# Tau-masked attention and a gated feed-forward on one core: 84 transposed tiles through the DMA crossbar instead of 70, shared staging buffers, one set of leads

## The chip, the cores and the metric

The kernel runs on one core of a Trainium2 chip. The metric is the time of one execution on the device in microseconds, the median of three runs. The kernel before takes 859.21 us (858.94 to 859.27).

## The reference

Eight batches, eight heads, 576 tokens, head size 64, all in float32. Cut to what matters:

```
scores = q @ k^T / 8                                   # per batch and head: 576 x 576
e      = where(scores >= max(scores) - tau, exp(scores - max), 0)
x      = (e / (sum(e) + 1e-9)) @ v                     # heads joined: 576 x 512 per batch
h      = relu(x @ w_in)                                # 512 -> 1024
c      = conv over tokens of h, 3 taps per channel
out    = (h * sigmoid(c)) @ w_out                      # 1024 -> 512
```

## The kernel before, in words

**Tiling.** The 576 queries of a batch are cut into four tiles of 128 and one of 64. Each batch has two chunks: the even chunk holds tiles 0 and 1, the odd chunk tiles 2, 3 and the small one, so there are 16 chunks. Heads go in four pairs per chunk. A unit (`unit`, L574) is one tile of one pair of heads; the small tiles of two neighbouring pairs are put together into one unit. That makes 8 units in an even chunk, 10 in an odd one, 18 in a batch and 144 in all; 128 of them are full tiles and 16 are small-tile units. "Half a chunk" below is the units of two pairs of heads, which end in one `attend`.

**One unit.** TensorE computes the scores of both heads into PSUM (L595). VectorE takes the row maximum (L607), ScalarE the exponential into the tile `em` (L614), VectorE the mask and the row sum (L617), and GpSimd, in one case of four ScalarE, the division (L655, L653). The keys lie along the columns of `em` and must come to the partitions before the product with v. This is done in one of two ways:

- `transposes` (L699): TensorE turns nine blocks of 128 x 128 in three groups of three (L710) into PSUM tiles `ps_t`, and ScalarE copies each group to the tile `eT` (L720). For a small-tile unit the two pairs have different `eT` tiles, so each group is copied in two halves (L726).
- `cross` (L671): the float32 words of `em` are split into their two 16-bit halves, one half by ScalarE and one by GpSimd (L363, L365), in a tile `parts`. SyncE's queue (SP) writes `parts` to a scratch tensor `rows` in DRAM (L688), and two transposing DMAs (called turns here, L695), one for each 64 rows of queries, bring them back into `eT` through the DMA crossbar.

Which way a unit goes is told by `crossed` (L666) from the table `CROSS`: for each pair of heads, the number of full tiles of a chunk that go through the crossbar (even chunks, odd chunks), and then whether the small-tile units go there. The first batch uses none. Before, that is one full tile of each pair in each chunk and all small-tile units: 10 units in a batch, 70 in all.

**Attend.** `attend` (L733) multiplies `eT` by v for two pairs of heads at a time, in two PSUM tiles of the same tag `ps_t`, and writes x (L754, L757). There are two `eT` buffers, one per pair, so the turns of the next two pairs wait until this product has read them.

**Feed-forward.** `ffn` (L839) gives the work of a finished chunk: `mm2` for blocks of 128 tokens (L827 into `po`, copied to the tile `ot` at L834, stored at L835), and `mm1` for each of eight slices of channels (L776 into `ph`, then relu, two taps, tanh and gate on ScalarE and VectorE). It is spread evenly over the units of the next chunk. What is left after the last unit ends the kernel.

**Weights.** `split` (L391) loads 16 pieces of 64-bit numbers in a `stage` buffer, converts them by way of a `value` buffer and writes a high and a low float32 part. This lies beside the first batch.

**The order.** All this is given to a planner on the host (`Plan`, L113). Each operation has a duration, a rank (its unit's number minus a lead) and its dependencies. `Plan.run` plays them on a model of the engines with a priority list and writes out one fixed order per engine; each engine then runs its order in sequence, and SP's queue does too. The leads are `AHEAD` by kind of work; `TRIM` adds to each of 12 kinds an amount for each of 16 chunks and the tail, read by `Lead` (L103). `LATENCY`, `HOLD`, `LATE`, `KEEP` and `SWITCH` are further costs of the model, `WRATE` is the rate at which weight pieces are ranked, and `BACKLOG` and `ALT` say when an operation may go to an engine other than its own. Buffers are handed out in turn: `STB`, `PTB`, `EMS`, `ETB` and `FAR` count those of `stage`, `parts`, `em`, `eT` and `rows`.

Of the kernel before, what the change touches and what calls it, by code (L numbers as in the profile page):

```python
# [22 lines left out]
AHEAD = {'mask': 5.447, 'norm': 7.929, 'parts': -2.68, 'gate': 1.222, 'evac': -0.535, 'low': 0.609, 's': 8.622, 's4': 8.87, 't': 3.177, 'a': 3.675, 'prep': 4.965, 'w': 1.618, 'load': 0.216, 'first': 3.806, 'ffn': 0.0}  # L23

TRIM = {
# [4 lines left out]
    'evac': (1.75, 1.55, -1.24, -3.99, -1.54, -1.06, 0.79, -0.48, -3.91, -4.07, -2.13, -3.07, -1.44, -1.08, -0.76, 0.84, 20.46),  # L30
    'mask': (-4.04, -1.01, 0.38, 3.13, -3.14, -4.4, -3.97, -4.18, -5.91, 0.85, 2.4, -3.79, 2.55, 0.33, -0.3, 4.2, 15.62),
    'parts': (9.64, -0.54, -1.96, -1.18, 0.42, 0.38, -0.86, 0.2, 4.19, 1.41, 3.28, -0.14, 1.44, 2.79, -0.77, 2.92, -20.75),
    'norm': (4.33, -3.3, -3.77, -0.77, 0.45, -1.05, 3.76, 0.73, -2.68, -1.39, 0.59, -0.77, -0.61, 3.7, -1.16, -2.44, 1.27),
    'gate': (-0.59, 0.08, -3.29, -0.05, -0.28, -0.05, 0.16, -0.15, -0.66, 0.11, -0.12, -0.14, -0.18, 0.76, -0.08, 1.88, -21.9),
    'low': (0.16, 0.28, -2.25, -1.71, -3.14, 3.41, 0.75, -0.39, -2.87, 2.41, -1.85, 2.2, -1.3, -0.19, -0.35, 4.7, 4.08),
    'prep': (-0.0, 0.01, 0.67, -1.53, 0.37, 1.4, 0.62, -0.62, -4.34, 0.86, -1.53, -0.82, -0.61, 1.13, -0.55, 1.19, -14.25),
    'ffn': (-4.93, 0.29, -0.2, -0.59, 0.59, -0.09, -0.24, -0.48, 0.08, -0.32, 0.15, 0.06, 0.45, -0.27, -0.0, 0.65, -9.58),
}
# [11 lines left out]
MOE = (3, 2)  # L50
BACKLOG = {'pool': 3000.0, 'dve': 3000.0, 'act': 9000000000.0}
WRATE = (1.713, 2.547)
ALT = 10.85
# [16 lines left out]
FAR = 4  # L70
# [32 lines left out]
class Lead:  # L103


    def __init__(self, plan):
        self.plan = plan

    def __getitem__(self, key):
        return AHEAD[key] + TRIM[key][self.plan.phase] if key in TRIM else AHEAD[key]  # L110


class Plan:  # L113
# [4 lines left out]
    def __init__(self):  # L118
        self.ops, self.wrote, self.read, self.bufs, self.tags, self.rank, self.phase = [], {}, {}, [], {}, 0.0, 0
# [160 lines left out]
def tile_tau_attention_gated_ffn(  # L280
# [48 lines left out]
    ahead_of = Lead(plan)  # L329
# [49 lines left out]
    def act(n, psum=False):  # L379
        return n * 0.833 + (58 if psum else 95)  # L380
# [10 lines left out]
    def split(src, n, name, high, low, hr, lr, first="load"):  # L391
# [3 lines left out]
        stage = plan.buf(wk, "stage", STB, [P, 1024], U32, name)  # L395
        value = plan.buf(wk, "value", 2, [P, 512], U32, f"{name}_f")
# [12 lines left out]
        w = ahead_of["w"]  # L409
# [20 lines left out]
        put(2 * n, load, issue=330, w=[hi, lo], r=[(gate, 0)] if first == "first" else [], ahead=w + ahead_of[first])  # L430
# [86 lines left out]
    def prep(i):  # L517
# [13 lines left out]
        a = ahead_of["prep"]  # L531
# [35 lines left out]
    def load_v(i, b, p):  # L567
        if b and chunks[pairs[i][0]].new[0]:
            return vts[i - NP]
        vt = plan.buf(wk, "v", VB, [P, NBLK, D], F32, f"v_{i}")  # L570
        put(NBLK * D, lambda: nc.sync.dma_start(vt[:], vc[b, p]), w=[(vt, 0)], r=[(gate, 0)] if i < NP else [], ahead=ahead_of["prep"])
        return vt

    def unit(u, sides, small):  # L574
# [7 lines left out]
        a = ahead_of["s4" if small else "s"]  # L582
# [48 lines left out]
        for h in range(m):  # L631
            op("dve", 738, late[h], w=[(em, h), (few, ("sum", h))], r=[(pss[h], 0), (few, "th")], ahead=a + ahead_of["mask"])
# [38 lines left out]
    def cross(u, em, dsts):  # L671

        parts = plan.buf(wk, "parts", PTB, [P, 2, 2 * S], U16, f"parts_{u}")
        rows = plan.buf(far, "rows", FAR, [2 * P, 2 * S], U16, f"rows_{u}")
        a = ahead_of["s"]
        for j in range(2):
            def part(e, j=j):
                src = em[:].bitcast(U16).rearrange("p (k two) -> p two k", two=2)[:, j]
                copy(e, parts[:, j], src)
# [3 lines left out]
            op(  # L683
                home, choice[home], part, w=[(parts, j)], r=[(em, 0), (em, 1)], ahead=a + ahead_of["parts"], port=True,
                other=[(e, ns) for e, ns in choice.items() if e != home]
            )
        put(
            864, lambda: nc.sync.dma_start(rows[:].rearrange("(q two) k -> q two k", two=2), parts[:]),  # L688
            w=[(rows, 0)], r=[(parts, 0), (parts, 1)], ahead=a, late=LATE["rows"]
        )  # L690
        for j in range(2):
            eT, g = dsts[j]

            def turn(j=j, eT=eT, g=g):
                nc.sync.dma_start_transpose(eT[:].bitcast(U16)[:, g], rows[j * P:(j + 1) * P, :])  # L695

            op("sp", 1560, turn, w=[(eT, (g, "x"))], r=[(rows, 0)], ahead=a, late=LATE["turn"], ring=1840)

    def transposes(u, em, dsts):  # L699
# [3 lines left out]
        def group(b0, n):  # L703
# [8 lines left out]
            op("pe", n * P * 0.852, turns, w=[(pt, 0)], r=[(em, 0), (em, 1), (ident, 0)], ahead=ahead_of["t"], kind="turn")  # L712
# [4 lines left out]
            if dsts[0][0] is dsts[1][0]:  # L717
# [15 lines left out]
    def attend(of, w, parts):  # L733

        pas = [plan.buf(ps_t, "ps_t", 2, [P, 512], F32, f"pa_{i}") for i, *_ in of]
        a = ahead_of["a"]
# [15 lines left out]
        for (i, p, eT, vt, x, off), pa in zip(of, pas):  # L752
# [6 lines left out]
            op("act", act(w, True), high, w=[(x, 0)], r=[(pa, 0)], ahead=a + ahead_of["low"])  # L759
            op("dve", dve(w), low, w=[(x, 1)], r=[(pa, 0), (x, 0)], ahead=a + ahead_of["low"])  # L760


    def mm1(c, f, xs):
# [23 lines left out]
        op("act", act(an, True), relu, w=[(hp, 0)], r=[(ph, 0), (hp.home, 0)], ahead=ahead_of["gate"])  # L787
        for j, k in enumerate((0, 2)):
# [4 lines left out]
            op("dve", dve(kn, 150), tap, w=[(t, 0)], r=[(hp, 0), (cr, 0)], ahead=ahead_of["gate"], port=True)  # L793
# [4 lines left out]
        op("act", act(kn) + 92, lambda: nc.scalar.activation(t[:, :kn], t[:, :kn], AF.Tanh, scale=cm[:, 0, f:f + 1]), w=[(t, 0)], r=[(cr, 0)], ahead=ahead_of["gate"])  # L798
        op("dve", dve(kn), gate, w=[(t, 0)], r=[(hp, 0)], ahead=ahead_of["gate"], port=True)
# [18 lines left out]
    def mm2(m):  # L818
# [4 lines left out]
        ot = plan.buf(wk, "ot", 2, [P, DO], F32, f"ot_{m}")  # L823
# [10 lines left out]
        op("act", act(DO, True), lambda: nc.scalar.activation(ot[:, :DO], po[:], AF.Copy), w=[(ot, 0)], r=[(po, 0)])  # L834
        put(DO, lambda: nc.sync.dma_start(tokens[m * P:(m + 1) * P, :], ot[:, :DO]), r=[(ot, 0)])  # L835
# [105 lines left out]
    plan.phase = len(chunks)  # L941
# [53 lines left out]
```

## Time and profile before

| | us |
|---|---|
| median of three runs | 859.21 (858.94 to 859.27) |
| the profiled execution | 857.69 |
| its span, first to last instruction | 855.9 |
| TensorE matmuls busy | 829.5 (97%) |
| TensorE weight loads busy (beside the matmuls) | 610.4 (71%) |
| VectorE busy | 725.4 (85%) |
| ScalarE busy | 659.3 (77%) |
| GpSimd busy | 407.3 (48%) |
| main DMA queue, share of 16 engines | 61.4% |
| granted TensorE clock, share of full speed | 1.0 in all slices |

Engines run side by side, so their times don't add up. Matmuls are pipelined: a row's duration overlaps the next one's, and what one costs the engine is the distance from its start to the start of the next. In the profile's names PE is TensorE, PEld its weight loads, DVE VectorE, ACT ScalarE, POOL GpSimd and SP SyncE. Traffic of the crossbar way: 576 KB written for each unit (70 of them) and 140 turns of 288 KB.

### The profile page before, as it was taken

Reading aid. Unit: us, or ns where it says so; the run is one execution under the profiler, and the core shown is the slowest. Engines: PE = TensorE matmul, PEld = TensorE weight load, DVE = VectorE, ACT = ScalarE, POOL = GpSimd, SP = SyncE. Lnnn points to the kernel's source line nnn. Section 1 sums busy time; section 2 is a strip of 40 time slices with the busy share of each in tenths; the row PEclk is TensorE's granted clock in tenths of the full one; section 3 lists DMA queues with packets and bytes.
Section 4 is the critical chain, followed back from the end, with each engine's and each line's share of the span. In section 5 each row is a group of like instructions: output and inputs, shape, how many; then the busy total and the mean of one; then the engine's idle time right before and its main releaser. Section 6 shows DMA issues by size and latency. Waiting matters only on the chain.

```text
span 855.9 us, 20930 instructions
## 1 busy us (share of the span) xinstructions
PE 829.5 (97%) x7710; PEld 610.4 (71%) x7710; DVE 725.4 (85%) x1869; ACT 659.3 (77%) x1300; POOL 407.3 (48%) x549
## 2 busy tenths in 40 slices
PE   6888999999999999999999999999999999999998
PEld 2545677767777677767777677776778677776896
DVE  6999889989899699987979879996979879997542
ACT  6999888877778678877878777896778768876642
POOL 3556545644537345553445445563553535554321
PEclk9999999999999999999999999999999999999999
DMA  8454247679667877668665686678665586645300
GB/s 274 152 169 153 75 120 180 170 206 206 167 145 178 216 185 189 167 184 226 164 161 130 199 200 163 150 210 229 154 167 154 167 221 176 151 124 152 80 26 37
DMA packets 213381, 140.72 MB, mean 164 GB/s; under 512 B 170400, under 2 KB 189088, under 8 KB 213280
## 3 DMA queue, kind: packets, MB, share of 16 engines
q1 hardware_dynamic: 212848, 139.09, 61.4%
q8 instruction: 61, 1.00, 0.5%
q10 hardware_dynamic: 432, 0.30, 0.1%
q14 instruction: 40, 0.33, 0.1%
HBM read 47.34 MB, written 50.72 MB: 115 GB/s over the span
## 4 chain that ended last, share of the span: by engine, by line
PE 86%; ACT 6%; DVE 5%; issue 1%; POOL 0%; DMA 0%; DVEq 0%; ACTq 0%
PE ph L776 23%; PE po L827 23%; PE ps_s L595 17%; PE pa L746 15%; PE ps_t L710 8%; ACT em L614 2%; DVE few L607 2%; DVE em L617 2%; ACT eT L720 1%; DVE t L791 1%; ACT stage_f L415 1%; PE pw_stage L441 0%; ACT stage L419 0%; DVE t L796 0%; DMA k<-in_kp_dram 0%
## 5 line engine op out<-in xcount | busy, mean ns | idle before, releaser
L655 POOL TENSOR_SCALAR em<-em,few 128x576 f32<-128x576 f32 x217 | 171.1, 796 | 215.1 <-DVE few L641 174.5
L607 DVE TENSOR_REDUCE few<-ps_s 128x1 f32<-128x576 f32 x288 | 209.2, 748 | 56.3 <-PE ps_s L595 54.4
L614 ACT ACTIVATE em<-ps_s,few 128x576 f32<-128x576 f32 x288 | 208.5, 747 | 61.7 <-DVE few L607 61.1
L617 DVE SCALAR_TENSOR_TENSOR em<-ps_s,few,em 128x576 f32<-128x576 f32 x288 | 224.9, 811 | 14.6 <-ACT em L614 7.5
L776 PE MATMUL ph<-x,w1h 128*128 128x322 f32 (+1 forms) x1024 | 237.0, 307 | 0.0
L370 POOL TENSOR_TENSOR gl<-t,gh 128x255 fp32r<-128x255 f32 (+9 forms) x192 | 121.0, 641 | 170.6 <-ACT gh L806 158.7
L776 PEld LDWEIGHTS ph<-x,w1h 128*128 128x128 f32 x1024 | 172.4, 189 | 21.4 <-issue 14.4
L595 PE MATMUL ps_s<-k,q 64*64 64x288 f32 x2048 | 163.8, 423 | 13.5 <-DVE em L617 8.3
L746 PE MATMUL pa<-eT,v 64*64 64x256 f32 (+1 forms) x2304 | 152.1, 403 | 0.0
L776 PE MATMUL ph<-x,w1l 128*128 128x322 f32 (+1 forms) x512 | 151.0, 295 | 0.0
L746 PEld LDWEIGHTS pa<-eT,v 64*64 64x64 f32 x2304 | 91.5, 133 | 48.6 <-issue 1.3
L827 PE MATMUL po<-w2h,gh 128*128 128x512 f32 x288 | 118.9, 413 | 0.0
L595 PEld LDWEIGHTS ps_s<-k,q 64*64 64x64 f32 x2048 | 67.3, 133 | 71.3 <-issue 29.5
L720 ACT ACTIVATE eT<-ps_t 128x384 f32<-128x384 f32 x216 | 101.6, 507 | 15.3 <-PE ps_t L710 15.0
L827 PE MATMUL po<-w2h,gl 128*128 128x512 f32 x288 | 112.7, 391 | 0.3 <-POOL gl L370 0.3
L827 PE MATMUL po<-w2l,gh 128*128 128x512 f32 x288 | 112.7, 391 | 0.0
L710 PE MATMUL ps_t<-ident,em 128*128 128x128 f32 x666 | 102.2, 280 | 7.0 <-POOL em L655 3.2
L710 PEld LDWEIGHTS ps_t<-ident,em 128*128 128x128 f32 x666 | 76.1, 141 | 39.5 <-ACT eT L720 11.7
L776 PEld LDWEIGHTS ph<-x,w1l 128*128 128x128 f32 x512 | 96.6, 189 | 0.4
L791 DVE SCALAR_TENSOR_TENSOR t<-hp,cr 128x321 f32<-128x321 f32 (+1 forms) x128 | 78.5, 614 | 19.4 <-ACT hp L785 18.5
L365 POOL COPY parts<-em 128x1152 uint16<-128x1152 uint16 x70 | 83.1, 1188 | 16.4 <-POOL em L655 5.5
L798 ACT ACTIVATE t<-t,cm 128x321 f32<-128x321 f32 (+1 forms) x128 | 68.4, 538 | 23.2 <-DVE t L791 16.4
(73 smaller groups left out, 941.9 us busy)
## 6 DMA issues: line engine op xcount, KB each, us to landing
rows<-parts SPq DMA_DIRECT2D x70, 576.0 KB, 3.6
q<-in_qd_dram SPq DMA_DIRECT2D x63, 256.0 KB, 3.4
v<-in_vc_dram SPq DMA_DIRECT2D x36, 288.0 KB, 4.3
out_dram<-ot SPq DMA_DIRECT2D x36, 256.0 KB, 3.1
k<-in_kp_dram SPq DMA_DIRECT2D x31, 288.0 KB, 4.0
stage<-in_w_in_dram SPq DMA_DIRECT2D x8, 512.0 KB, 4.9
stage<-in_w_out_dram SPq DMA_DIRECT2D x8, 512.0 KB, 3.9
eT<-rows SPq DMA_TRANSPOSE x140, 4.2
```

What stands on the lines that cost most here:

```text
L370: engines[e].tensor_tensor(dst, x, y, op=ALU.subtract)
L595: nc.tensor.matmul(ps[g * D:(g + 1) * D, AT + c * CH:AT + (c + 1) * CH], lhsT=q(on, h), rhs=k[on, h * CH:(h + 1) * CH], start=True, stop=True)
L607: nc.vector.tensor_reduce(few[:, nm], scores(), op=ALU.max, axis=mybir.AxisListType.XY, negate=True)
L614: nc.scalar.activation(view(), scores(), AF.Exp, bias=few[:, nm])
L617: nc.vector.scalar_tensor_tensor(view(), scores(), few[:, th], view(), op0=ALU.is_ge, op1=ALU.mult, accum_out=few[:, total])
L655: engines[e].tensor_scalar(sl, sl, LEAST, few[:, 10 + h:11 + h], op0=ALU.add, op1=ALU.mult)
L710: nc.tensor.transpose(out=pt[:, i * P:(i + 1) * P], in_=block, identity=ident[:])
L720: "act", act(n * P, True), lambda: nc.scalar.activation(eT[:, g:g + 2, b0:b0 + n, :], source(), AF.Copy),
L746: nc.tensor.matmul(pa[j * D:(j + 1) * D, :w], lhsT=vt[on, step, :], rhs=eT[on, :w // D, step, :], start=(step == 0), stop=(step == NBLK - 1))
L776: nc.tensor.matmul(ph[:, :an], lhsT=w1[w][:, cb, fs], rhs=xs[cb][:, h, :an], start=(cb == 0 and i == 0), stop=(cb == NCB - 1 and i == 2))
L791: nc.vector.scalar_tensor_tensor(t[:, :kn], hp[:, o + k:o + kn + k], cr[:, j, f:f + 1], y, op0=ALU.mult, op1=ALU.add)
L827: nc.tensor.matmul(po[:], lhsT=x[:, f, at:at + P], rhs=w[:, f, :], start=(f == 0 and i == 0), stop=(f == NFB - 1 and i == 2))
```

## The change: what it does

- `CROSS`: two full tiles of every first and third pair of heads and one of every second and fourth go through the crossbar, and no small-tile unit does. That is 12 units in a batch, 84 in all, all of them full tiles.
- The tile `parts` has no buffer of its own (before: one); it takes one of the three `stage` buffers, which grow from 1024 to 1152 words. The output tile `ot` takes a `value` buffer; these become three (before: two of `value`, two of `ot`).
- `rows` has three scratch tensors instead of four.
- `TRIM`, `Lead` and the lead `ffn` go; every lead has one value for the whole kernel. All other numbers of the planner have new values, so the order of work on every engine is a new one.

```diff
-AHEAD = {'mask': 5.447, 'norm': 7.929, 'parts': -2.68, 'gate': 1.222, 'evac': -0.535, 'low': 0.609, 's': 8.622, 's4': 8.87, 't': 3.177, 'a': 3.675, 'prep': 4.965, 'w': 1.618, 'load': 0.216, 'first': 3.806, 'ffn': 0.0}
-TRIM = {
-    's': (-0.17, 0.37, 0.28, -0.24, -0.45, -0.1, -0.02, -0.17, -0.17, -0.23, -0.12, -0.0, -0.27, 0.06, 0.05, 1.05, -19.16),
...
-LATENCY = {'pe': 205.37, 'act': 213.173, 'dve': 118.588, 'pool': 62.545, 'ring': 1882.404}
-HOLD = {'pool': 134.468, 'dve': 107.493}
+AHEAD = {'mask': 10.551, 'norm': 10.168, 'parts': -3.787, 'gate': 1.873, 'evac': 0.451, 'low': 0.345, 's': 8.614, 's4': 9.392, 't': 3.022, 'a': 3.819, 'prep': 6.275, 'w': 1.364, 'load': 0.901, 'first': 5.447}
+LATENCY = {'pe': 228.875, 'act': 210.482, 'dve': 115.463, 'pool': 47.975, 'ring': 1863.104}
+HOLD = {'pool': 114.519, 'dve': 83.078}
...
-MOE = (3, 2)
-BACKLOG = {'pool': 3000.0, 'dve': 3000.0, 'act': 9000000000.0}
-WRATE = (1.713, 2.547)
-ALT = 10.85
+MOE = (2, 1)
+BACKLOG = {'pool': 1000000000.0, 'dve': 0.0, 'act': 9000000000.0}
+WRATE = (2.137, 2.121)
+ALT = 4.72
...
-FAR = 4
+FAR = 3
...
-PTB = 1
+VAB = 3
 QB = 2
-CROSS = ((1, 1, 1, 1), (1, 1, 1, 1), (1, 1))
-LATE = {'load': 1319.0, 'copy': 4674.0, 'rows': 335.0, 'turn': -88.0}
-KEEP = {'rows': 3.322, 'cols': 0.012, 'turn': 0.252, 'full': 0.371}
+CROSS = ((2, 1, 2, 1), (2, 1, 2, 1), (0, 0))
+LATE = {'load': 1337.0, 'copy': 13931.0, 'rows': -123.0, 'turn': 157.0}
+KEEP = {'rows': 3.335, 'cols': 0.001, 'turn': 0.103, 'full': 0.266}
...
-        stage = plan.buf(wk, "stage", STB, [P, 1024], U32, name)
-        value = plan.buf(wk, "value", 2, [P, 512], U32, f"{name}_f")
+        stage = plan.buf(wk, "stage", STB, [P, 2 * S], U32, name)
+        value = plan.buf(wk, "value", VAB, [P, 512], U32, f"{name}_f")
...
-        parts = plan.buf(wk, "parts", PTB, [P, 2, 2 * S], U16, f"parts_{u}")
+        parts = plan.buf(wk, "stage", STB, [P, 2 * S], U32, f"parts_{u}")
...
-        ot = plan.buf(wk, "ot", 2, [P, DO], F32, f"ot_{m}")
+        ot = plan.buf(wk, "value", VAB, [P, DO], U32, f"ot_{m}")
...
-            plan.rank -= ahead_of["ffn"]
```

## Rows read from the trace of the kernel before

**Rows 1.** Stages, busy us of each engine (instructions), then clock, DMA share, GB/s.

```profile
0.00:105.00 105.00, 85.80 (x786) 52.61 (x787) 92.32 (x248) 91.68 (x184) 54.19 (x73) 1.00 0.52 168
105.00:800.00 695.00, 691.52 (x6596) 513.19 (x6595) 610.53 (x1580) 545.63 (x1064) 338.87 (x456) 1.00 0.68 175
800.00:856.00 56.00, 52.21 (x334) 44.62 (x332) 22.55 (x42) 21.96 (x54) 14.22 (x21) 1.00 0.07 25
...
204.00:302.00 98.00, 97.23 (x916) 71.88 (x915) 85.00 (x214) 73.15 (x144) 46.48 (x62) 1.00 0.73 177
...
700.00:800.00 100.00, 99.10 (x945) 75.10 (x946) 87.64 (x225) 77.10 (x154) 49.69 (x69) 1.00 0.61 157
```

**Rows 2.** The chain that ended last, share of the span by engine and line.

```profile
PE 86%; ACT 6%; DVE 5%; issue 1%; POOL 0%; DMA 0%; DVEq 0%; ACTq 0%
PE ph L776 23%; PE po L827 23%; PE ps_s L595 17%; PE pa L746 15%; PE ps_t L710 8%; ACT em L614 2%; DVE few L607 2%; DVE em L617 2%; ACT eT L720 1%; DVE t L791 1%; ACT stage_f L415 1%; PE pw_stage L441 0%; ACT stage L419 0%; DVE t L796 0%; DMA k<-in_kp_dram 0%
```

**Rows 3.** Waits in us (times, longest), TensorE over the span, VectorE in 105:800.

```profile
PE ps_s L595 <- DVE em L617: 9.6, 11, 2.2
...
DVE few L607 <- PE ps_s L595: 51.9, 43, 5.4
```

**Rows 4.** Timeline of TensorE around groups of transposes: start us, us.

```profile
418.67 0.87 PE L710 MATMUL ps_t<-ident,em 128*128 128x128 f32 x6
419.30 0.48 PE L827 MATMUL po<-w2h,gh 128*128 128x512 f32 x1
...
437.19 0.82 PE L710 MATMUL ps_t<-ident,em 128*128 128x128 f32 x6
437.94 1.20 PE L595 MATMUL ps_s<-k,q 64*64 64x288 f32 x16
439.08 0.55 PE L710 MATMUL ps_t<-ident,em 128*128 128x128 f32 x3
439.38 0.39 PE L776 MATMUL ph<-x,w1h 128*128 128x322 f32 x1
```

**Rows 5.** Groups of instructions: busy us, mean ns, idle before and releasers.

```profile
L655 POOL TENSOR_SCALAR em<-em,few 128x576 f32<-128x576 f32 x217 | 171.1, 796 | 215.1 <-DVE few L641 174.5 <-PE ps_s L595 19.1 <-PE ps_t L710 9.1
...
L710 PE MATMUL ps_t<-ident,em 128*128 128x128 f32 x666 | 102.2, 280 | 7.0 <-POOL em L655 3.2 <-ACT eT L720 2.4 <-DMA q<-in_qd_dram 1.2
L720 ACT ACTIVATE eT<-ps_t 128x384 f32<-128x384 f32 x216 | 101.6, 507 | 15.3 <-PE ps_t L710 15.0
...
L365 POOL COPY parts<-em 128x1152 uint16<-128x1152 uint16 x70 | 83.1, 1188 | 16.4 <-POOL em L655 5.5 <-DMA rows<-parts 2.5 <-issue 2.5
L363 ACT ACTIVATE parts<-em 128x1152 uint16<-128x1152 uint16 x70 | 81.6, 1165 | 1.6 <-POOL em L655 1.4
...
L726 ACT ACTIVATE eT<-ps_t 128x192 f32<-128x192 f32 x12 | 3.6, 393 | 0.0
```

**Rows 6.** Timeline of GpSimd and VectorE around one half of a tile's parts.

```profile
419.89 1.21 POOL L365 COPY parts<-em 128x1152 uint16<-128x1152 uint16 x1
...
417.63 0.47 DVE L791 SCALAR_TENSOR_TENSOR t<-hp,cr 128x255 f32<-128x255 f32 x1
...
420.09 1.29 DVE L791 SCALAR_TENSOR_TENSOR t<-hp,cr,t 128x255 f32<-128x255 f32 x1
```

**Rows 7.** Instructions of the weights' staging: ns min/median/max, first and last start us.

```profile
L428 POOL TENSOR_TENSOR stage_f<-stage_f,stage x16: 1284/1298/1466, 17.2 to 91.3; 128x512 int32<-128x512 int32 x16
```

**Rows 8.** Two attends in the chain, in order of time: start us, us.

```profile
407.22 4.84 PE pa L746 x72
...
424.11 3.89 PE pa L746 x72
```

**Rows 9.** SP's queue between these attends, and the turns' landing over the span.

```profile
412.10 3.02 SPq L695 DMA_TRANSPOSE eT<-rows  x2
...
415.85 3.52 SPq L695 DMA_TRANSPOSE eT<-rows  x2
...
DMA to landing us min/median/max: 3.4/4.2/6.4
```

More of the change, by code (lines that the diff above doesn't have):

```diff
@@ L100 @@
 Chunk = collections.namedtuple("Chunk", "b tiles new cols tokens done")
[L103 to L110, printed above, removed]
 class Plan:
     def __init__(self):
-        self.ops, self.wrote, self.read, self.bufs, self.tags, self.rank, self.phase = [], {}, {}, [], {}, 0.0, 0
+        self.ops, self.wrote, self.read, self.bufs, self.tags, self.rank = [], {}, {}, [], {}, 0.0
     def buf(self, pool, tag, bufs, shape, dtype, name):
@@ L389, in pool1, with split @@
         return n * 0.9 + 225
-    def split(src, n, name, high, low, hr, lr, first="load"):
-        stage = plan.buf(wk, "stage", STB, [P, 1024], U32, name)
-        value = plan.buf(wk, "value", 2, [P, 512], U32, f"{name}_f")
+    def split(src, n, name, high, low, hr, lr, lead="load"):
+        stage = plan.buf(wk, "stage", STB, [P, 2 * S], U32, name)
+        value = plan.buf(wk, "value", VAB, [P, 512], U32, f"{name}_f")
         def flat():
@@ L408, in split @@
         lo, hi, a = (stage, 0), (stage, 1), (value, 0)
-        w = ahead_of["w"]
+        w = AHEAD["w"]
         def load():
@@ L428, in f4 @@
             nc.gpsimd.tensor_tensor(v(I32), v(I32), words(I32)[0], op=ALU.add)
-        put(2 * n, load, issue=330, w=[hi, lo], r=[(gate, 0)] if first == "first" else [], ahead=w + ahead_of[first])
+        put(2 * n, load, issue=330, w=[hi, lo], r=[(gate, 0)] if lead == "first" else [], ahead=w + AHEAD[lead])
         op("act", act(n), f0, w=[a], r=[hi], ahead=w)
@@ L530, in prep @@
         q = plan.buf(wk, "q", QB, [P, 2, w], F32, f"q_{i}")
-        a = ahead_of["prep"]
+        a = AHEAD["prep"]
         after = [(gate, 0)] if i < NP else []
@@ L570, in load_v @@
         vt = plan.buf(wk, "v", VB, [P, NBLK, D], F32, f"v_{i}")
-        put(NBLK * D, lambda: nc.sync.dma_start(vt[:], vc[b, p]), w=[(vt, 0)], r=[(gate, 0)] if i < NP else [], ahead=ahead_of["prep"])
+        put(NBLK * D, lambda: nc.sync.dma_start(vt[:], vc[b, p]), w=[(vt, 0)], r=[(gate, 0)] if i < NP else [], ahead=AHEAD["prep"])
         return vt
@@ L581, in unit @@
         few.home = fews[few.turn % FEW]
-        a = ahead_of["s4" if small else "s"]
+        a = AHEAD["s4" if small else "s"]
         late, pss = [], []
@@ L631, in unit @@
         for h in range(m):
-            op("dve", 738, late[h], w=[(em, h), (few, ("sum", h))], r=[(pss[h], 0), (few, "th")], ahead=a + ahead_of["mask"])
+            op("dve", 738, late[h], w=[(em, h), (few, ("sum", h))], r=[(pss[h], 0), (few, "th")], ahead=a + AHEAD["mask"])
         ss = [(few, ("sum", h)) for h in range(m)]
@@ L671, in cross, with halves @@
     def cross(u, em, dsts):
-        parts = plan.buf(wk, "parts", PTB, [P, 2, 2 * S], U16, f"parts_{u}")
+        parts = plan.buf(wk, "stage", STB, [P, 2 * S], U32, f"parts_{u}")
+        def halves():
+            return parts[:].bitcast(U16).rearrange("p (j k) -> p j k", j=2)
         rows = plan.buf(far, "rows", FAR, [2 * P, 2 * S], U16, f"rows_{u}")
-        a = ahead_of["s"]
+        a = AHEAD["s"]
         for j in range(2):
@@ L678, in part @@
                 src = em[:].bitcast(U16).rearrange("p (k two) -> p two k", two=2)[:, j]
-                copy(e, parts[:, j], src)
+                copy(e, halves()[:, j], src)
             choice = {"act": act(2 * S), "pool": pool1(2 * S), "dve": dve(2 * S)}
@@ L683, in cross @@
             op(
-                home, choice[home], part, w=[(parts, j)], r=[(em, 0), (em, 1)], ahead=a + ahead_of["parts"], port=True,
+                home, choice[home], part, w=[(parts, j)], r=[(em, 0), (em, 1)], ahead=a + AHEAD["parts"], port=True,
                 other=[(e, ns) for e, ns in choice.items() if e != home]
@@ L687, in cross @@
         put(
-            864, lambda: nc.sync.dma_start(rows[:].rearrange("(q two) k -> q two k", two=2), parts[:]),
+            864, lambda: nc.sync.dma_start(rows[:].rearrange("(q two) k -> q two k", two=2), halves()),
             w=[(rows, 0)], r=[(parts, 0), (parts, 1)], ahead=a, late=LATE["rows"]
@@ L710, in turns @@
                     nc.tensor.transpose(out=pt[:, i * P:(i + 1) * P], in_=block, identity=ident[:])
-            op("pe", n * P * 0.852, turns, w=[(pt, 0)], r=[(em, 0), (em, 1), (ident, 0)], ahead=ahead_of["t"], kind="turn")
+            op("pe", n * P * 0.852, turns, w=[(pt, 0)], r=[(em, 0), (em, 1), (ident, 0)], ahead=AHEAD["t"], kind="turn")
             def source():
@@ L720, in group @@
                     "act", act(n * P, True), lambda: nc.scalar.activation(eT[:, g:g + 2, b0:b0 + n, :], source(), AF.Copy),
-                    w=[(eT, (g, b0))], r=[(pt, 0)], ahead=ahead_of["t"] + ahead_of["evac"]
+                    w=[(eT, (g, b0))], r=[(pt, 0)], ahead=AHEAD["t"] + AHEAD["evac"]
                 )
@@ L726, in group @@
                         "act", act(n * D, True), lambda j=j, eT=eT, g=g: nc.scalar.activation(eT[:, g, b0:b0 + n, :], source()[:, j], AF.Copy),
-                        w=[(eT, (g, b0))], r=[(pt, 0)], ahead=ahead_of["t"] + ahead_of["evac"]
+                        w=[(eT, (g, b0))], r=[(pt, 0)], ahead=AHEAD["t"] + AHEAD["evac"]
                     )
@@ L735, in attend @@
         pas = [plan.buf(ps_t, "ps_t", 2, [P, 512], F32, f"pa_{i}") for i, *_ in of]
-        a = ahead_of["a"]
+        a = AHEAD["a"]
         read = parts + [(y[3], 0) for y in of]
@@ L757, in low @@
                 nc.vector.tensor_tensor(x[:, 1, off:off + w], pa[:, :w], x[:, 0, off:off + w].bitcast(F32), op=ALU.subtract)
-            op("act", act(w, True), high, w=[(x, 0)], r=[(pa, 0)], ahead=a + ahead_of["low"])
-            op("dve", dve(w), low, w=[(x, 1)], r=[(pa, 0), (x, 0)], ahead=a + ahead_of["low"])
+            op("act", act(w, True), high, w=[(x, 0)], r=[(pa, 0)], ahead=a + AHEAD["low"])
+            op("dve", dve(w), low, w=[(x, 1)], r=[(pa, 0), (x, 0)], ahead=a + AHEAD["low"])
     def mm1(c, f, xs):
@@ L785, in relu @@
             nc.scalar.activation(hp[:, 1:1 + an], ph[:, :an], AF.Relu, scale=0.5)
-        op("act", act(an, True), relu, w=[(hp, 0)], r=[(ph, 0), (hp.home, 0)], ahead=ahead_of["gate"])
+        op("act", act(an, True), relu, w=[(hp, 0)], r=[(ph, 0), (hp.home, 0)], ahead=AHEAD["gate"])
         for j, k in enumerate((0, 2)):
@@ L833, in mm2 @@
             op("pe", 691, mm, w=[(po, 0)], r=gs + [(w, (f, i)) for w in w2 for i in range(0, DO, WN)], kind="full")
-        op("act", act(DO, True), lambda: nc.scalar.activation(ot[:, :DO], po[:], AF.Copy), w=[(ot, 0)], r=[(po, 0)])
-        put(DO, lambda: nc.sync.dma_start(tokens[m * P:(m + 1) * P, :], ot[:, :DO]), r=[(ot, 0)])
+        op("act", act(DO, True), lambda: nc.scalar.activation(ot[:, :DO].bitcast(F32), po[:], AF.Copy), w=[(ot, 0)], r=[(po, 0)])
+        put(DO, lambda: nc.sync.dma_start(tokens[m * P:(m + 1) * P, :], ot[:, :DO].bitcast(F32)), r=[(ot, 0)])
     tokens = out.rearrange("b s d -> (b s) d")
@@ L938, in tile_tau_attention_gated_ffn @@
             plan.rank, fn = work.pop(0)
-            plan.rank -= ahead_of["ffn"]
             fn()
-    plan.phase = len(chunks)
     for _, fn in work + ffn(len(chunks)):
```

19 lines of the change are left out of this document (4 added, 15 removed), and 3 rows, old and new, of the table TRIM.

## The prediction

> **What bounds the kernel now.** I read the busy times by stage first. Three stages have different limits [rows 1]. In the first 105 us, batch 0 and the weights, TensorE is busy 85.8 us, so it stands idle 19.2, while VectorE (92.3) and ScalarE (91.7) are nearly full. From 105 to 800 us, where batches 1 to 7 run, TensorE is busy 691.5 of 695 us: 3.5 us idle in all. From 800 us only feed-forward is left, and TensorE idles 3.8 us at the end. Then the chain that ended last: 86% of it is TensorE's own work, 8% of the span being the transposes [rows 2]. Last the waits: VectorE waits 51.9 us for scores in the middle stage, while TensorE's longest wait for VectorE is 9.6 us over the whole span [rows 3]. So the middle stage is set by how much work TensorE is given, and the others follow it. The clock is 1.00 in every stage [rows 1] and does not enter.
>
> The Trainium skill ("Perfetto Trace Analysis", Identifying the Most-Contended Engine) says that matmul busy time is a poor measure of how near TensorE is to its limit, and wants weight loads judged instead. By that the middle stage is at 513 of 695 us, 74%, and the matmuls taken away would buy nothing. The starts of successive matmuls leave no gap here, so I side with the chain; the rule's case comes back as a rival.
>
> **Transposes on TensorE.** Units that TensorE transposes fall from 74 to 60: 44 full tiles and all 16 small ones, against 72 and 2. At nine each that is 540 instead of the 666 of [rows 5], 126 fewer. The mean of 280 ns there is a pipelined duration; the price is the distance between starts [rows 4]: three transposes take 439.38 - 439.08 = 0.30 us, six take 419.30 - 418.67 = 0.63 us, so 100 to 105 ns each. With scores next, six take 437.94 - 437.19 = 0.75 us, 125 ns each. A removed group mostly stands between other work whose change of shape remains, so I take 102.5 ns: 126 x 0.1025 = 12.9 us, between 12.6 and 15.8. All of it is in the middle stage, and nearly all on the path.
>
> **ScalarE and GpSimd.** 84 copies of 507 ns go (216 to 132: -42.6 us), 84 half copies of 393 ns come (12 to 96: +33.0), and 14 halves of `parts` at 1165 ns come (+16.3) [rows 5]: ScalarE +6.7 us on 545.6 in the middle [rows 1]. GpSimd gets 14 x 1.188 = +16.6 us on 338.9. Both have over 140 us of room there and cost nothing while TensorE stays the last to finish. VectorE gets no new work, but an L791 step beside a `parts` copy on GpSimd took 1.29 us against 0.47 [rows 6], so I count up to 14 x 0.82 = 11.5 us: 622 of the 682 us left, 91% against 88% now. TensorE's backlog covers that; without the cover the whole 11.5 us would come back.
>
> **SP and the crossbar.** 14 more units bring 14 writes and 28 turns to SP's queue. Two turns occupy it 3.0 to 3.5 us [rows 9], so about 14 x 3.3 = 46 us more over 682, beside loads that stand in the same queue. The DMA engines are at 0.68 over the middle stage, 473 us [rows 1]. If everything there were crossbar traffic, a unit would be 473/70 = 6.8 us; at the head's rate (168 GB/s at share 0.52, so 323 GB/s when full) its 1.18 MB would be 3.7 us. So 14 units add 51 to 95 us and the share becomes 0.77 to 0.83. That is room still, and the stretch with share 0.73 leaves TensorE 0.8 us idle in 98, the one with 0.61 leaves 0.9 in 100 [rows 1]: up to here TensorE does not feel it. I take nothing, with the rival below as the other end.
>
> The small-tile units, last of their half chunk, now reach `eT` by TensorE and a half copy instead of a write and a turn, whose turn alone lands after 4.2 us [rows 9]. That eases the attends of odd chunks. In even chunks each half now needs six turns instead of four, and since `eT` has one buffer per pair they can start only after the attend before.
>
> **Buffers.** `parts` gets up to three buffers instead of one; the waits for the single one (2.5 us on GpSimd [rows 5]) lie off the path. The weights have left `stage` by 91.3 + 1.3 us [rows 7], and no unit before batch 1 uses the crossbar, so they hardly meet; outputs meet the weights in `value` even less. Three `rows` tensors are just the three units of a half chunk. All this I put at zero, between -1 and +1 us.
>
> **Edits that change nothing.** `MOE`: the list of `ffn` has put all blocks but one of `mm2` first, then the last, then `mm1`, whatever the pair. `LATE['copy']` is read nowhere. `BACKLOG` and `ALT`: of 218 divisions whose own engine is GpSimd, 217 ran there [rows 5], so hardly anything was moved.
>
> **The new order.** The trims can have improved only what was idle. In the middle that is 3.5 us at present; a perfect order would give back these 3.5, and an order as loose as the head (18% idle) would cost over 100. The middle is nearer, since the same backlog of feed-forward stands ready there, but one set of leads has less to fit with: I let the idle time double, +3.5 us. In the head weight pieces are asked for at other rates; there VectorE and ScalarE bind, and their work is the same: 0, between -4 and +6. The end is TensorE's own row of matmuls: 0.
>
> **The sum.** 857.69 (profiled execution: span 855.9 and 1.8 around it) - 12.9 + 3.5 = 848.3. The median of the runs is 859.21, 1.5 above the profiled one, so 849.8 us. Its own range: 846 to 855.
>
> **Rivals.**
>
> *Late attends (slower).* The place is the gap between the attend that ends at 407.22 + 4.84 = 412.1 and the one at 424.1 [rows 8]. Four turns go out, the last begins near 417.6 and lands near 421.8 by the median 4.2 us [rows 9], 2.3 us before its reader. Two more turns take 3.3 us, so the attend would be 1 us late, and later as the DMA share grows. TensorE runs in order, so an attend at the front of its queue holds everything. It decides from 12.9 / 28 = 0.46 us of waiting per attend of batches 1 to 7. At 0.8 us each it costs 22.4: 857.7 - 12.9 + 22.4 + 1.5 = 868.7 us. For it: the 2.3 us. Against it: no attend waits for a turn now, and the planner may place attends later, since the four gaps of a batch have about 99 - 18 = 81 us together and need some 15 each. The Trainium skill ("VectorE: DVE Perf Modes", Rules for kernel authors) speaks for it: it sends a 128 x 128 transpose to TensorE where PSUM will do, to the crossbar otherwise. The 60 x 9 transposes that stay follow it; the 14 moved units go against it.
>
> *VectorE takes the place (no change).* In the head VectorE is 88% busy and TensorE waits. If 622 us of VectorE cannot be packed closer than about 89.5%, the middle stays at 695 us and the time at 859 (855 to 861 with the packing a little off). For it: the head. Against it: VectorE's 51.9 us of waits for scores, and 87.6 of 100 us with such waits among them [rows 1, 3]. This is also the case in which the skill's weight-load rule would be right.
>
> *A loose order (slower).* Without trims TensorE idles 3% of the middle stage, 20 us: 857.7 - 12.9 + 17 + 1.5 = 863 us. For it: 204 numbers go. Against it: the backlog.
>
> *More than forecast.* Each removed group takes its change of shape with it (15.8 us), idle time stays as it is, and the head gains 4: 857.7 - 15.8 - 4 + 1.5 = 839.4; with only part of this 840 to 846.
>
> **How the numbers follow.** Forecast 0.50, more than forecast 0.16, VectorE 0.12, late attends 0.13, loose order 0.09. A measurement of this kernel tells 0.2% (1.7 us) from none, so faster means below 857.5: 0.50 + 0.16 + 0.02 of the VectorE case = 0.68; within 857.5 to 860.9: 0.08 of it and 0.01 of the loose order = 0.09; slower: 0.13 + 0.08 + 0.02 = 0.23. The range from 842 to 866 leaves out about 0.07 below and 0.10 above. The predicted time is 849.8 us.
>
> **What would show it.** 540 transposes with starts 100 to 105 ns apart; 96 half copies and 84 of each `parts` row; a middle stage shortened by 8 to 13 us with TensorE idle under 8 us in it; DMA share 0.77 to 0.83. Late attends would show as waits of L746 or its weight loads for a transposing DMA, the VectorE case as TensorE's scores waiting for L617 by over 10 us in the middle, the loose order as idle time of TensorE spread over many releasers. The prediction is wrong if the middle stage does not shrink, or if the head's 105 us change by more than 6.

## The result, and the profile after

The changed kernel takes 844.26 us (842.77 to 844.64, four runs) against 859.08 for the one before on the same chip: a ratio of 0.9824 [0.9807, 0.9841], 14.8 us less. The forecast was 849.8, the range 842 to 866. The direction and the range held; the time came out 1.7 us below the forecast's own range of 846 to 855, where the rival "more than forecast" stands. The profiled execution took 844.64 us, 13.05 less than the one before.

The stages of the changed kernel, columns as in [rows 1]; the last line is a piece of the head:

```profile
0.00:105.00 105.00, 86.56 (x750) 50.32 (x751) 93.33 (x237) 88.16 (x175) 53.55 (x72) 0.97 0.50 166
105.00:800.00 695.00, 692.75 (x6634) 509.72 (x6633) 628.70 (x1609) 555.80 (x1108) 366.52 (x482) 1.00 0.78 199
800.00:843.00 43.00, 39.00 (x205) 34.42 (x203) 14.90 (x25) 14.53 (x31) 8.77 (x10) 1.00 0.08 31
...
40.00:60.00 20.00, 17.18 (x118) 9.14 (x117) 18.30 (x53) 17.22 (x34) 9.04 (x10) 0.83 0.53 183
```

In the head TensorE is busy about as long as before (86.6 us for 85.8). Between 105 and 800 us TensorE is idle 2.25 us, less than the 3.5 of [rows 1], and does more of its work there, so that 43 us are left after 800 instead of 56. The DMA share is 0.78. In the head of this execution TensorE's clock stood at 1.2 instead of 2.4 GHz for 6.8 us, after a stretch in which TensorE idled for 1.8 of 4 us between transposes (44 to 48 us; the row of 40 to 60 shows the mean clock, 0.83). Of the four runs the only one at full clock throughout was the fastest, 842.77, against 844.2 to 844.6, so the spell costs about 1.6 us here.

The chain that ended last and the groups that answer to [rows 2] and [rows 5] (line numbers are smaller, since the trims are gone):

```profile
PE 89%; ACT 5%; DVE 4%; issue 1%; DMA 0%; POOL 0%; DVEq 0%; ACTq 0%
PE ph L754 24%; PE po L805 24%; PE ps_s L569 18%; PE pa L724 16%; PE ps_t L688 7%; DVE few L581 1%; ACT em L588 1%; ACT eT L698 1%; DVE em L591 1%; ACT stage_f L389 1%; ACT stage L393 1%; DMA k<-in_kp_dram 0%; ACT k L337 0%; ACT w1h L410 0%; ACT w2h L410 0%
...
L724 PE MATMUL pa<-eT,v 64*64 64x256 f32 (+1 forms) x2304 | 152.2, 403 | 0.7 <-ACT eT L704 0.7
...
L339 POOL COPY parts<-em 128x1152 uint16<-128x1152 uint16 x84 | 100.8, 1200 | 29.1 <-issue 18.6 <-POOL em L629 8.1
L337 ACT ACTIVATE parts<-em 128x1152 uint16<-128x1152 uint16 x84 | 98.1, 1168 | 1.2 <-POOL em L629 0.9
...
L688 PE MATMUL ps_t<-ident,em 128*128 128x128 f32 x540 | 85.4, 285 | 7.7 <-ACT eT L698 3.7 <-POOL em L629 2.5 <-DMA q<-in_qd_dram 0.6
...
L698 ACT ACTIVATE eT<-ps_t 128x384 f32<-128x384 f32 x132 | 61.1, 498 | 11.4 <-PE ps_t L688 11.2
...
L704 ACT ACTIVATE eT<-ps_t 128x192 f32<-128x192 f32 x96 | 25.8, 348 | 8.3 <-PE ps_t L688 8.2
```

The counts are the forecast ones: 540 transposes, 132 and 96 copies, 84 of each half of the parts. TensorE's share of the chain rose from 86% to 89%: nothing took the place of the transposes.

The attends on TensorE's timeline (start us, us), at the same place of a batch as in [rows 8]:

```profile
403.63 5.03 PE L724 MATMUL pa<-eT,v 64*64 64x320 f32 x72
426.71 1.48 PE L724 MATMUL pa<-eT,v 64*64 64x256 f32 x24
```

SP's queue between them, and the landing of all turns over the span, as in [rows 9]:

```profile
408.69 10.47 SPq L673 DMA_TRANSPOSE eT<-rows  x6
```
```profile
DMA to landing us min/median/max: 3.7/4.3/6.4
```

Six turns go out in one row, 1.75 us each. The last begins near 417.4 and lands near 421.7; the next attend starts at 426.7. The new order put 18 us between these two attends where there were 12, and fed TensorE from the backlog meanwhile. Over the span the attends wait 0.7 us in all, for a half copy of ScalarE (the row of L724 above) and never for a turn. So the attends are not late.

**What a change of shape costs.** Scores and attends use TensorE in blocks of 64 rows and columns, transposes and feed-forward whole. The traces show what a change between the two costs. In this stretch of the changed kernel eight score matmuls stand first between attend steps, then between feed-forward steps:

```profile
524.87 0.67 PE L569 MATMUL ps_s<-k,q 64*64 64x288 f32 x8
525.35 0.61 PE L724 MATMUL pa<-eT,v 64*64 64x256 f32 x8
...
530.81 0.71 PE L569 MATMUL ps_s<-k,q 64*64 64x288 f32 x8
531.46 0.41 PE L754 MATMUL ph<-x,w1h 128*128 128x322 f32 x1
...
532.15 0.31 PE L754 MATMUL ph<-x,w1l 128*128 128x322 f32 x1
532.30 0.46 PE L754 MATMUL ph<-x,w1h 128*128 128x322 f32 x2
532.60 0.31 PE L754 MATMUL ph<-x,w1l 128*128 128x322 f32 x1
```

And three feed-forward matmuls alone between scores, elsewhere on the same timeline:

```profile
141.24 0.41 PE L754 MATMUL ph<-x,w1h 128*128 128x322 f32 x1
141.49 0.31 PE L754 MATMUL ph<-x,w1l 128*128 128x322 f32 x1
141.64 0.31 PE L754 MATMUL ph<-x,w1h 128*128 128x322 f32 x1
141.88 0.71 PE L569 MATMUL ps_s<-k,q 64*64 64x288 f32 x8
```

From start to start the eight scores take 0.48 us in their own shape and 0.65 us amid the other: +0.17. Three feed-forward matmuls take 0.45 us in a run (532.15 to 532.60) and 0.64 alone between scores (141.24 to 141.88): +0.19. Two changes cost 0.36 us, so one costs 0.18. The other places of this kind in the middle stage agree: eight scores between attend steps take 0.485 us (median of 15), amid feed-forward 0.646 (median of 4). Counted from the order of the matmuls in the traces there are 263 changes before and 267 after.

### The profile page after: what moved, and what is told of

Read it like the earlier page. It is cut to its first block, busy times and chain, and to the rows that moved or that the text cites. A ratio compares the mean times of both kernels' runs of the same rounds, so it can differ in the third digit from the quotient of the medians.

```text
span 842.6 us, 20783 instructions
## 1 busy us (share of the span) xinstructions
PE 818.3 (97%) x7584; PEld 594.5 (71%) x7584; DVE 736.9 (87%) x1869; ACT 658.5 (78%) x1313; POOL 428.8 (51%) x564
## 4 chain that ended last, share of the span: by engine, by line
PE 89%; ACT 5%; DVE 4%; issue 1%; DMA 0%; POOL 0%; DVEq 0%; ACTq 0%
PE ph L754 24%; PE po L805 24%; PE ps_s L569 18%; PE pa L724 16%; PE ps_t L688 7%; DVE few L581 1%; ACT em L588 1%; ACT eT L698 1%; DVE em L591 1%; ACT stage_f L389 1%; ACT stage L393 1%; DMA k<-in_kp_dram 0%; ACT k L337 0%; ACT w1h L410 0%; ACT w2h L410 0%
## 5 line engine op out<-in xcount | busy, mean ns | idle before, releaser
L591 DVE SCALAR_TENSOR_TENSOR em<-ps_s,few,em 128x576 f32<-128x576 f32 x288 | 225.3, 811 | 14.9 <-ACT em L588 8.4
L754 PE MATMUL ph<-x,w1h 128*128 128x322 f32 (+1 forms) x1024 | 231.0, 304 | 0.5 <-ACT hp L763 0.5
L344 POOL TENSOR_TENSOR gl<-t,gh 128x255 fp32r<-128x255 f32 (+9 forms) x192 | 124.1, 658 | 132.1 <-ACT gh L784 126.4
L724 PE MATMUL pa<-eT,v 64*64 64x256 f32 (+1 forms) x2304 | 152.2, 403 | 0.7 <-ACT eT L704 0.7
L724 PEld LDWEIGHTS pa<-eT,v 64*64 64x64 f32 x2304 | 91.2, 133 | 49.6 <-issue 2.4
L569 PEld LDWEIGHTS ps_s<-k,q 64*64 64x64 f32 x2048 | 66.6, 134 | 71.7 <-issue 25.8
L339 POOL COPY parts<-em 128x1152 uint16<-128x1152 uint16 x84 | 100.8, 1200 | 29.1 <-issue 18.6
L769 DVE SCALAR_TENSOR_TENSOR t<-hp,cr 128x321 f32<-128x321 f32 (+1 forms) x128 | 82.5, 645 | 21.7 <-ACT hp L763 20.5
L337 ACT ACTIVATE parts<-em 128x1152 uint16<-128x1152 uint16 x84 | 98.1, 1168 | 1.2 <-POOL em L629 0.9
L688 PE MATMUL ps_t<-ident,em 128*128 128x128 f32 x540 | 85.4, 285 | 7.7 <-ACT eT L698 3.7
L688 PEld LDWEIGHTS ps_t<-ident,em 128*128 128x128 f32 x540 | 62.0, 143 | 42.2 <-issue 17.6
L769 DVE SCALAR_TENSOR_TENSOR t<-hp,cr,t 128x321 f32<-128x321 f32 (+1 forms) x128 | 87.2, 682 | 0.3
```

Source lines behind the costliest of these rows:

```text
L339: engines[e].tensor_copy(dst, src)
L344: engines[e].tensor_tensor(dst, x, y, op=ALU.subtract)
L569: nc.tensor.matmul(ps[g * D:(g + 1) * D, AT + c * CH:AT + (c + 1) * CH], lhsT=q(on, h), rhs=k[on, h * CH:(h + 1) * CH], start=True, stop=True)
L591: nc.vector.scalar_tensor_tensor(view(), scores(), few[:, th], view(), op0=ALU.is_ge, op1=ALU.mult, accum_out=few[:, total])
L688: nc.tensor.transpose(out=pt[:, i * P:(i + 1) * P], in_=block, identity=ident[:])
L724: nc.tensor.matmul(pa[j * D:(j + 1) * D, :w], lhsT=vt[on, step, :], rhs=eT[on, :w // D, step, :], start=(step == 0), stop=(step == NBLK - 1))
```

## The experiments

Each run is compared with the kernel before on its own chip. "Span", "idle" and "half clock" are those of the profiled execution. "Idle" is the span less the time in which matmuls are busy, "changes" are the changes of shape, "half clock" is the time within the span for which TensorE was granted 1.2 instead of 2.4 GHz. "Sum" adds to the changed kernel's span what the transposes (0.109 us each, worked out below), the changes (0.18 us each) and the idle time differ from its own; it leaves the clock out.

| kernel | transposes | changes | idle us | half clock us | span us | sum us | median us | ratio to before |
|---|---|---|---|---|---|---|---|---|
| before | 666 | 263 | 26.4 | 0 | 855.9 | 857.7 | 859.1 | 1 |
| changed | 540 | 267 | 24.3 | 6.8 | 842.6 | 842.6 | 844.3 | 0.9824 [0.9807, 0.9841] |
| 1: 70 units, new order | 666 | 283 | 26.2 | 6.8 | 862.5 | 861.1 | 863.3 | 1.0058 [1.0041, 1.0075] |
| 2: 84 units, old order and buffers | 540 | 319 | 36.0 | 10.2 | 871.4 | 863.7 | 869.8 | 1.0140 [1.0111, 1.0168] |
| 3: 126 transposes more | 666 | 319 | 28.4 | 0 | 866.6 | 869.8 | 868.6 | 1.0114 [1.0094, 1.0135] |
| 4: before, no trims | 666 | 271 | 24.8 | 6.8 | 857.8 | 857.5 | 859.0 | 1.0008 [0.9996, 1.0020] |
| 5: changed, own parts buffer | 540 | 309 | 37.9 | 13.7 | 868.7 | 863.8 | 870.2 | 1.0121 [1.0102, 1.0140] |
| 6: 84 units, old leads, shared buffers | 540 | 293 | 31.5 | 3.4 | 854.3 | 854.5 | 858.2 | 0.9989 [0.9979, 0.9999] |
| 7: 70 units, fitted | 666 | 275 | 24.8 | 0 | 856.5 | 858.2 | 858.4 | 0.9994 [0.9984, 1.0003] |
| 8: 98 units | 414 | 353 | 54.3 | 17.1 | 888.6 | 874.4 | 891.6 | 1.0375 [1.0352, 1.0397] |
| 9: 84 units, own buffer, fitted | 540 | 335 | 30.4 | 3.4 | 861.2 | 860.9 | 863.7 | 1.0072 [1.0053, 1.0091] |
| 10: changed, fewer changes | 540 | 255 | 26.2 | 3.4 | 841.3 | 842.3 | 843.8 | 0.9843 [0.9828, 0.9858] |
| 11: changed, six em buffers | 540 | 273 | 23.9 | 3.4 | 840.5 | 843.3 | 843.6 | 0.9837 [0.9822, 0.9852] |

**1. The old table in the changed kernel.**

```diff
-CROSS = ((2, 1, 2, 1), (2, 1, 2, 1), (0, 0))
+CROSS = ((1, 1, 1, 1), (1, 1, 1, 1), (1, 1))
```

> The changed kernel with the old table of 70 crossbar units; all planner numbers, buffers and leads of the changed kernel stay. Theory (TensorE's own work sets the middle stage, a transpose is worth 102.5 ns): 126 transposes come back, 12.9 us, so 857 us (855 to 860), with 666 transposes and under 6 us of TensorE idle time between 105 and 800 us. Rival (the new order made the gain): 844 to 849 us, although the transposes are back.

19 us come back, not 12.9. So the gain hangs on the table, and the new order alone makes none (the rival falls); but more comes back than my price. TensorE's idle time grew by 1.9 us only; 16 more changes of shape are 2.9 us.

**2. The new table in the kernel before.** The same edit the other way.

> The kernel before with the new table of 84 crossbar units alone; trims, leads, the single parts buffer and four rows tensors stay. Theory: -12.9 us from 859.1, so 846 us (844 to 850). Rival (the new order or the shared buffers are needed for the gain): 854 us or more, with TensorE idle over 8 us between 105 and 800 us, waiting for attends or for the single parts buffer.

Slower than before by 1.4%: my theory falls. The middle stage by engine, columns as in [rows 1]:

```profile
105.00:800.00 695.00, 681.17 (x6341) 489.30 (x6343) 612.74 (x1569) 536.65 (x1056) 355.99 (x460) 1.00 0.75 195
```

TensorE is idle 13.8 us in it. Its row of the waits there (us in total, times, longest) that answers to the 2.5 us of [rows 5]:

```profile
POOL parts L365 <- DMA rows<-parts: 28.0, 20, 3.4
```

GpSimd waits for the single parts buffer to be written out. No matmul waits for it by name. One piece of the chain that ended last in this run, and TensorE's row right behind it (start us, us; in brackets the idle time before and what ended it):

```profile
326.74 4.92 DMA rows<-parts
...
331.76 1.16 ACT parts L363
332.92 0.76 ACT em L653
333.68 0.64 ACT em L614
...
334.34 1.56 DVE em L617 x4
```
```profile
335.31 0.72 PE L595 MATMUL ps_s<-k,q 64*64 64x288 f32 x8 [0.89 <-DVE em L617]
```

When the write has landed, ScalarE starts its half of the next parts. Behind it in ScalarE's order stand a division and exponentials, VectorE's mask waits for an exponential, and TensorE's next scores wait 0.89 us for the mask. Such writes are 10.5 us of the chain in this run, and none of it in the kernel before or the changed one. So the wait stands off TensorE's path by name and reaches it through a queue. How much of the 13.8 us comes about in this way is not shown: by name TensorE waits most for VectorE's mask, 15.0 us over the span against the 9.6 of [rows 3].

**3. 126 transposes more in the changed kernel.** The third group of each TensorE-turned unit after batch 0 runs twice.

```diff
+            again = 2 if u >= 18 and b0 == 2 * BLOCKS else 1
-                for i in range(n):
+                for i in [*range(n)] * again:
-            op("pe", n * P * 0.852, turns, ...
+            op("pe", n * P * 0.852 * again, turns, ...
```

> The changed kernel; of each TensorE-turned unit of batches 1 to 7 (42 of them) the third group of three transposes is issued twice into the same PSUM tile, so 126 transposes more with no further copy and no other work; the planner knows their duration. Theory (price 102.5 ns each and no slack on TensorE): +12.9 us, so 857 us (855.5 to 859). Rival (the price is that of the distance with changes of shape, 125 to 137 ns): 860 to 862. Rival (VectorE already sets part of the middle stage): under 852.

+24.4 us, above both prices. The trace has 319 changes of shape instead of 267, 9.4 us, and 4.1 us more idle time: the planner's order, fitted to the kernel without them, came out worse. 13.7 + 9.4 + 4.1 makes 27.2, 3.2 more than the two spans differ; 1.6 of that is the spell at half clock, which the changed kernel's execution had and this one had not. The time rose by more than TensorE's added work and nothing of it was absorbed, so the rival with VectorE falls.

**4. The kernel before without trims.** `Lead` returns `AHEAD[key]`.

> The kernel before with all trims at zero (one set of leads, its own); 70 crossbar units. Theory (trims can only win idle time of TensorE, of which a steady backlog leaves little): 859 to 864 us. Rival (one set of leads costs much, and the changed kernel paid it back elsewhere): over 866 us, with TensorE idle over 10 us in the middle stage.

1.0008 [0.9996, 1.0020]: 204 trims, or their loss, make no difference that these runs can tell.

**5. The changed kernel with one buffer for the parts.**

```diff
-        parts = plan.buf(wk, "stage", STB, [P, 2 * S], U32, f"parts_{u}")
+        parts = plan.buf(wk, "parts", 1, [P, 2 * S], U32, f"parts_{u}")
```

> The changed kernel (84 units, its own planner numbers) with a single buffer for the parts, as before, in place of the three shared ones. Theory (the single buffer holds the em tiles back and so breaks the order up): 855 us or more, with waits of the parts copies for the writing DMA of over 15 us and over 290 changes between 64-row and 128-row matmuls on TensorE (267 in the changed kernel). Rival (the buffers lie off the path, as the prediction had it): 843 to 848 us.

26 us slower: the whole gain goes, and 11 us more. The wait of experiment 2 is back, and TensorE is idle 15.6 us in the middle stage (row of the waits, then row of the stage):

```profile
POOL parts L339 <- DMA rows<-parts: 24.3, 22, 3.3
```
```profile
105.00:800.00 695.00, 679.38 (x6413) 485.67 (x6412) 616.70 (x1574) 540.75 (x1064) 353.26 (x466) 1.00 0.76 196
```

**6. Old leads and trims, 84 units, shared buffers.** Experiment 2 with `parts` in `stage`, `ot` in `value` and three `value` buffers, as in the change.

> The kernel before with its leads and trims, but 84 units and the shared stage and value buffers of the changed kernel; four rows tensors. Theory (what the old order lacked for 84 units was the buffers): 12 us or more below the 869.8 of the old order with a single parts buffer, so at most 858. Rival (the leads and trims, fitted to 70 units, were what failed): 865 us or more.

11.6 us less than experiment 2, at the edge of what was asked (858.2 against "at most 858"). The wait of the parts copies for the write is gone. Its span is 11.7 us longer than the changed kernel's: 26 changes of shape (4.7) and 7.2 us of idle time. I put these down to the fit of the order; it has one `rows` tensor more besides, which no run tried by itself.

**7. 70 units, shared buffers, leads fitted anew.** Experiment 1 with other `AHEAD`, `WRATE`, `LATE` and `KEEP` values.

> The changed kernel with 70 units, as in the first experiment, but with leads, late costs, keep values and weight rates fitted anew to 70 units. Theory (a transpose is worth 109 ns of TensorE by the distance of groups of three from groups of six, 126 of them 13.7 us, once the order suits the table): 856 to 859 us. Rival (a well-fitted order makes the gain, whatever the table): 850 us or less.

858.4: as expected. A fitted order with 70 units and three parts buffers is as fast as the kernel before with one; neither the buffers nor the fit buy anything there. Against it the changed kernel saves 14 us by the medians. At full clock the spans are 856.5 and 840.9, 15.6 us apart: 13.7 for 126 transposes, 1.4 for eight changes of shape and 0.5 of idle time.

**8. 98 units.** `CROSS = ((2, 2, 2, 1), (2, 2, 2, 1), (0, 0))`.

> The changed kernel with 98 crossbar units (two tiles of three pairs of four), planner numbers unchanged. Theory (fewer transposes always pay): -13.7 us from the changed kernel, 831 us. Rival (late attends: up to eight turns between two attends, three rows tensors for four units): 855 us or more, with TensorE idle over 10 us between 105 and 800 us and DMA share over 0.80.

4% slower (two runs), with fewer transposes than ever; the middle stage by engine, and the longest wait of its matmuls:

```profile
105.00:800.00 695.00, 666.72 (x6054) 466.18 (x6054) 597.61 (x1518) 526.26 (x1007) 364.17 (x466) 0.99 0.83 211
```
```profile
PE ph L754 <- ACT hp L763: 17.5, 12, 3.0
```

The rival's numbers came, but not its mechanism: no matmul of an attend is seen waiting for a turn. TensorE is idle 28 us there, and for 17.5 of them it waits for ScalarE to copy the feed-forward's `ph`. The changes of shape are 86 more than in the changed kernel, about 15 us. The leads are those fitted to 84 units; as in experiment 1, an order that was made for another table may be what fails. So it is shown that fewer transposes alone don't pay, and not shown that the crossbar, the three `rows` tensors or the DMA share of 0.83 set a limit at 98 units.

**9. One parts buffer, leads fitted anew to it.**

> 84 units with a single buffer for the parts, as in the fifth experiment, with leads, late costs, keep values and weight rates fitted anew to it. Theory (a single buffer limits 84 units whatever the leads): 853 us or more, still with waits of the parts copies for the writing DMA of over 15 us and over 290 changes of shape. Rival (only the leads were unsuited, the buffers lie off the path): 848 us or less.

863.7, still slower than before, with the parts copies waiting for the write, in the row of its waits:

```profile
POOL parts L339 <- DMA rows<-parts: 36.3, 22, 4.0
```

Writes of the parts are 10.2 us of its chain. So experiment 5 was no accident of unsuited leads: with one parts buffer 84 units did not pay in any of the three orders tried (experiments 2, 5 and 9).

**10 and 11. Two more fits of the changed kernel.** Ten has other leads and 255 changes; eleven adds a sixth `em` buffer.

> The changed kernel with other leads, weight rates, late and keep values: the same work, with 255 changes between 64-row and 128-row matmuls on TensorE instead of 267. Theory (0.19 us for a change, idle time as it is): -2.3 us from the changed kernel, 842 us (840.5 to 843.5). Rival (the changes cost nothing of their own and only go along with idle time): 844 us or more.

> The changed kernel with six em buffers in the space that sharing set free, and leads, rates, late and keep values fitted to it; 273 changes of shape. Theory (TensorE is busy nearly all of the middle stage, so buffers for work ahead of it win nothing more): 843 to 846 us. Rival (VectorE and ScalarE gain a lead that pays, above all in the head): under 841 us.

Both ratios overlap the changed kernel's. In ten the 2.2 us of fewer changes are given back as 1.9 us of idle time, so its theory fails as put: the idle time did not stay, and the run does not settle the price of a change. Eleven has 694.0 of 695 us busy in the middle stage and gains nothing that can be told. No version beats the changed kernel by more than the runs can tell.

## Why the prediction was right, and where it was off

- **What bounds the kernel**: right. The middle stage is TensorE's work before and after, and experiment 7 against the changed kernel shows it with both orders fitted. The last attend ends at 794 us instead of 809, that of batch 0 at 125 instead of 123: batches 1 to 7 take 17 us less, where 8 to 13 were forecast. The Trainium skill ("Perfetto Trace Analysis", Identifying the Most-Contended Engine) judges TensorE's headroom by weight loads and by the arithmetic achieved. By the weight loads alone, as the prediction read it, there would have been no gain; they stood at 73% of the middle stage, and the time fell.
- **Price of a transpose**: 12.9 us was 0.8 too low. [Rows 4] held the better number: six take 0.63 us and three 0.30 us between the same neighbours, scores before and feed-forward behind, so three more take 0.33 (0.328 by the trace), 0.109 each, 13.7 us. I had divided a group's time by three, although by these rows a group of three takes some 0.03 us less than three such prices. That changes of shape remain was right: 267 against 263.
- **The new order**: the term that was most off. I added 3.5 us for idle time; it fell by 2.1. With the transposes (-13.7) and four changes of shape (+0.7) that makes -15.1. The two executions at full clock, 857.69 and 842.77, differ by 14.9; the two profiled ones by 13.05, since the changed kernel's had its spell at half clock.
- **The clock, and the 1.5 us**: "does not enter" was wrong. I took 1.5 us between the profiled run and the median as given. Of the executions of the kernel before that ran beside the experiments, 16 had a mean granted clock of 1.000 and took 857.7 us (median), 19 had 0.998 and took 859.4. The profiled execution before was one without a spell; by its time, for its clock is not on record, the median of 859.21 is one of executions with one. The changed kernel's median stands 1.5 above its execution at full clock too (844.26 and 842.77). The term was right, for a reason that I had not seen.
- **Buffers at zero**: wrong as a reason. The waits for the one parts buffer, 2.5 us and off the path at 70 units, are 24 to 36 us on GpSimd at 84, and the writes stand in the chain that ended last (10.5 and 10.2 us in experiments 2 and 9, none before). By my reasoning the change would have gained as much with one buffer; experiment 5 measured 870.2 us. That the forecast came out in spite of this is luck: the change happens to bring the buffers that make it pay.
- **Trims, and the edits that change nothing**: the trims are shown to be worth nothing that can be told in the kernel before (experiment 4). `MOE`, `BACKLOG` and `LATE['copy']` were not tried one by one; 218 of 218 divisions ran on GpSimd.
- **Other engines**: DMA share 0.78 (0.77 to 0.83 forecast). GpSimd rose by 21.5 us (16.6 forecast), VectorE by 11.5, the bound given for copies on GpSimd beside it. ScalarE stayed (658.5 us, +6.7 forecast): a half copy took 348 ns, not 393, and half copies overlap, so that 96 of them keep it busy for 25.8 us, 22.2 more than before where 33.0 were forecast.
- **Rivals**: late attends did not come; the order had moved the attend (18 us instead of 12). VectorE at 90% of the middle stage (628.7 of 695) did not take the place. The Trainium skill's rule for TensorE against the crossbar ("VectorE: DVE Perf Modes", Rules for kernel authors) does not hold for these 14 units with TensorE at its limit and three parts buffers: with these on the crossbar the kernel took 1.8% less time. At 98 units the kernel was slower, but in an order that was not fitted to them, so that run speaks neither for the rule nor against it.

## What to carry to other kernels

On a bound engine, price an operation by the distance from n to 2n of them between the same neighbours, and count changes of shape as work of their own. Ask of every buffer that a change uses more often whether an in-order engine waits for it, and what the bound engine needs from behind that wait. And compare structures only after the order is fitted to each: one edit of a table moved this kernel by +11 or -14 us, depending on buffers and fit.

## What the runs showed that was not expected

- A change between 64-row and 128-row matmuls costs TensorE 0.18 us, by this estimate 48 us over the 267 of the changed kernel, and hides in its busy time: experiment 3 has 19.9 us more of it than the changed kernel for 13.7 us of transposes.
- For nine kernels the sum of transposes, changes and idle time meets the span within 3.2 us. For 2, 5 and 8, the three with the most idle time, it falls short by 5 to 14 us. They are also the only ones with spells at half clock in the middle stage, so that they have 3.4, 6.8 and 10.2 us more of it than the changed kernel. At half the clock a spell can cost at most half its length, 1.7, 3.4 and 5.1 us; where the rest of the shortfall lies stays open.
- TensorE's clock fell to 1.2 GHz for 3.4 to 6.8 us in the head of the profiled execution of most of these kernels, the changed one among them. It did not in that of the kernel before [rows 1], yet other executions of that kernel have a spell too, as their granted clock of 0.998 and their 1.7 us more show. So the spell comes in some executions of a kernel and not in others, and two profiled executions are to be compared with it in view.
